# Decode step with cached attention beside a gated MLP: w4 loaded between the last V and wo, the gate folded into the head outputs, the second branch added on the PE

## Chip, cores, metric

One core of one Trainium2 chip. The metric is the device time of one execution in microseconds (us), lower is better. Every time below is of a run within 1.5% of the fastest of the same kernel. Kernels of one group of experiments ran on the same chip and share the runs of the kernel before.

## The reference, cut to what matters

```python
x = A_x                                                 # 2 x 1 x 1024, bf16
g = sigmoid((x * gate_w).sum(-1, keepdims=True))
# A: one query per head over a cache; B=2, H=32, Sk=16384, Dh=128
q = (x @ wq) as 32 heads
p = softmax(q . k_cache * Dh**-0.5)
a = (p . v_cache) as 4096 columns @ wo                  # wo 4096 x 1024
# B: a mixer and an MLP on the same x
x1 = x + shift(gelu(layernorm(x) @ w1)) @ w2            # 1024 x 1024 each
b  = x1 + gelu(layernorm(x1) @ w3) @ w4                 # w3 1024 x 3584, w4 3584 x 1024
return g * a + (1 - g) * b
```

The two caches are 268 MB each, the weights together 36 MB. Every byte is read once, and the output is 4 KB.

## The kernel before

All large loads go through one pool of three buffers of 64 KB per partition. A step of the attention (one batch element, two heads) takes one 8 MB K tile and one 8 MB V tile, 32 of each. The weights of the second branch take a turn in the same ring after steps 4, 8 and 16; wo comes last, in pieces.

```python
const = ctx.enter_context(tc.tile_pool(name="const", bufs=1))
big = ctx.enter_context(tc.tile_pool(name="big", bufs=NBIG))        # NBIG = 3
tpool = ctx.enter_context(tc.tile_pool(name="tpool", bufs=2))
# ... more pools behind them ...
V_SPLIT_LAST = [NJ // 2, NJ // 4, NJ // 8, NJ // 8]                 # NJ = 256
WO_SPLIT = [4] * 6 + [2, 2, 1, 1, 1, 1]                             # rows of wo, 256 KB each
# ...
def wo_stage():
    Q1 = const.tile([P, B, 32], BF16)
    # ... transposes OT, permutes it on the PE into Q (also a const tile) ...
    for r in range(32):
        for c in range(KC):                                         # KC = 8
            nc.tensor.matmul(wo_acc[:, c, :], lhsT=wo[:, r, :, c], rhs=Q[:, :, r],
                             start=(r == 0 and c == 0), stop=(r == 31 and c == KC - 1))
# ...
def st_down():                                                      # at step 16
    nc.vector.tensor_tensor(out=pre[:], in0=x1[:], in1=linear("w4", h2T)[:], op=ALU.add)
    nc.vector.tensor_tensor(out=pre[:], in0=pre[:], in1=over_r(omg_bc[:]), op=ALU.mult)
# ... the end:
fin = const.tile([P, KC, B], FP32)
nc.vector.tensor_tensor(out=fin[:], in0=wo_acc[:], in1=over_r(g_bc[:]), op=ALU.mult)
out_pm = const.tile([P, B, KC], BF16)
nc.vector.tensor_tensor(out=out_pm[:].rearrange("p b r -> p r b"), in0=fin[:], in1=pre[:], op=ALU.add)
```

Pools lie behind one another in each partition, in the order in which they are opened.

Of the kernel before, what the change touches and what calls it, by code (L numbers as in the profile page):

```python
# [10 lines left out]
FP32 = mybir.dt.float32  # L11
BF16 = mybir.dt.bfloat16
ACTF = mybir.ActivationFunctionType
ALU = mybir.AluOpType
# [9 lines left out]
def kernel(  # L24
# [15 lines left out]
    nc = tc.nc  # L40
    P = nc.NUM_PARTITIONS
    B, Sq, D = A_x.shape
# [3 lines left out]
    G = 2  # L46
    NJ = G * Sk // P
# [4 lines left out]
    KC = D // P  # L52
    FC = F // P
    scale = float(Dh) ** -0.5
    NHG = H // G
    NT = B * NHG
# [3 lines left out]
    const = ctx.enter_context(tc.tile_pool(name="const", bufs=1))  # L60
    big = ctx.enter_context(tc.tile_pool(name="big", bufs=NBIG))
# [8 lines left out]
    def misc_psum(shape, dtype=FP32):  # L70
        return mps.tile(shape, dtype, tag="misc", name="misc")

    def big_tile(name):
        return big.tile([P, SLOT], BF16, tag="big", name=name)
# [7 lines left out]
    kn_tiles = {}  # L82
    vn_tiles = {}
    wt = {}
    V_SPLIT_LAST = [NJ // 2, NJ // 4, NJ // 8, NJ // 8]

    def cache_rows(cache, i):
        b, hg = tiles[i]
# [11 lines left out]
    def load_v(i):  # L100
# [3 lines left out]
        j0 = 0  # L104
        for n in V_SPLIT_LAST if i == NT - 1 else [NJ]:
            nc.sync.dma_start(out=tv[:, j0 : j0 + n, :], in_=src[:, j0 : j0 + n, :])
# [3 lines left out]
    def load_rows(keys, srcs):  # L110

        t = big_tile("wt")
        c0 = 0
        for key, src in zip(keys, srcs):
            R, N = src.shape[0] // P, src.shape[1]
            v = t[:, c0 : c0 + R * N].rearrange("p (r n) -> p r n", n=N)
            nc.sync.dma_start(out=v, in_=src.rearrange("(p r) n -> p r n", p=P))
            wt[key] = v
            c0 += R * N


    WO_SPLIT = [4] * 6 + [2, 2, 1, 1, 1, 1]

    def load_wo():
        t = big_tile("wo")[:].rearrange("p (r n) -> p r n", n=D)
        src = A_wo.rearrange("(p r) n -> p r n", p=P)
        r0 = 0
        for n in WO_SPLIT:
            nc.sync.dma_start(out=t[:, r0 : r0 + n, :], in_=src[:, r0 : r0 + n, :])
            r0 += n  # L130
        wt["wo"] = t


    x_pm = const.tile([P, B, KC], BF16)
# [2 lines left out]
    def load_first():  # L137
# [7 lines left out]
    ident_f = const.tile([P, P], FP32)  # L145
# [4 lines left out]
        out=perm[:].rearrange("k (h a) -> k h a", a=4),  # L150
        in_=ident_f[:].rearrange("k (a h) -> k h a", a=4),
# [24 lines left out]
    for g in range(1, 4):  # L176
        nc.vector.tensor_tensor(
            out=osel_f, in0=osel_f, in1=ident_f[:, 40 * g : 40 * g + 8], op=ALU.add
# [4 lines left out]
    for v in range(4):  # L183
        nc.gpsimd.affine_select(
            out=selv[:, v],
            in_=selv[:, v],
# [21 lines left out]
    def total(src):  # L208

        ps = misc_psum([P, src.shape[1]])  # L210
        nc.tensor.matmul(ps[:], lhsT=ones_f[:], rhs=src, start=True, stop=True)  # L211
        return ps

    def over_r(v):

        return v.unsqueeze(1).to_broadcast([P, KC, B])


    g_bc = const.tile([P, B], FP32)
# [62 lines left out]
    OT = const.tile([P, B, H], BF16)  # L282
    wo_acc = acc.tile([P, KC, B], FP32, name="wo_acc")
# [56 lines left out]
    def pv_rows(V, PT, oc):  # L340



        O = ops.tile([P, 4 * Dh], FP32, name="O")
        for m in range(NM):
            for g in range(4):
                j0 = m * CJ + 4 * g
                nc.tensor.matmul(  # L348
                    O[32 * g : 32 * g + 32, :],
                    lhsT=PT[:, m : CJ * 32 : 16],  # L350
                    rhs=V[:, j0 : j0 + 4, :],
                    start=(m == 0),
                    stop=(m == NM - 1),
                )
        Os = ppool.tile([P, 4, Dh], FP32, tag="PrOs", name="Os")
        nc.scalar.copy(out=Os[:].rearrange("p x d -> p (x d)"), in_=O[:])  # L356
        for x in range(4):
            nc.tensor.matmul(  # L358
                oc[:], lhsT=Os[:, x, :], rhs=osel[:, x, :], start=(x == 0), stop=(x == 3)
            )  # L360

    def pv_stage(i):
        b, hg = tiles[i]
        PT = PT_tiles.pop(i)
        rs = rs_tiles.pop(i)
        V = vn_tiles.pop(i)[:].rearrange("p (j d) -> p j d", d=Dh)
        rs2 = stat.tile([P, G], FP32, name="rs2")
        nc.vector.tensor_scalar(  # L368
            out=rs2[:], in0=hmask[:], scalar1=rs[:, 0:1], scalar2=None, op0=ALU.mult
        )  # L370
        rinv = stat.tile([P, G], FP32, name="rinv")
        nc.vector.reciprocal(out=rinv[:], in_=total(rs2[:])[:])  # L372
        oc = misc_psum([P, G])
        pv_rows(V, PT, oc)
        nc.vector.tensor_tensor(  # L375
            out=OT[:, b, hg * G : (hg + 1) * G], in0=oc[:], in1=rinv[:], op=ALU.mult
        )

    def wo_stage():


        Q1 = const.tile([P, B, 32], BF16)
        for b in range(B):
            nc.vector.transpose(out=Q1[:, b, :], in_=OT[:, b, :])
        q_ps = misc_psum([P, B, 32])
        nc.tensor.matmul(q_ps[:], lhsT=perm[:], rhs=Q1[:], start=True, stop=True)
        Q = const.tile([P, B, 32], BF16)
        nc.vector.tensor_copy(out=Q[:], in_=q_ps[:])
        wo = wt.pop("wo").rearrange("k r (p c) -> k r p c", c=KC)
        for r in range(32):  # L390
            for c in range(KC):
                nc.tensor.matmul(
                    wo_acc[:, c, :],
                    lhsT=wo[:, r, :, c],
                    rhs=Q[:, :, r],
                    start=(r == 0 and c == 0),
                    stop=(r == 31 and c == KC - 1),
                )
# [38 lines left out]
    def linear(key, actT):  # L437

        w = wt.pop(key)
        R, C = w.shape[1], w.shape[2] // P  # L440
        ps = misc_psum([P, C, B])
        for c in range(C):
            for r in range(R):
                nc.tensor.matmul(  # L444
                    ps[:, c, :],
                    lhsT=w[:, r, :].rearrange("k (p c) -> k p c", c=C)[:, :, c],
                    rhs=actT[:, r, :],
                    start=(r == 0),
                    stop=(r == R - 1),
                )  # L450
        return ps
# [4 lines left out]
    x1 = const.tile([P, KC, B], FP32)  # L456
    xn2T = const.tile([P, KC, B], BF16)
    h2T = const.tile([P, FC, B], BF16)
    pre = const.tile([P, KC, B], FP32)
# [17 lines left out]
        gelu(h2[:], h2T[:], FC)  # L477

    def st_down():
        nc.vector.tensor_tensor(out=pre[:], in0=x1[:], in1=linear("w4", h2T)[:], op=ALU.add)  # L480
        nc.vector.tensor_tensor(out=pre[:], in0=pre[:], in1=over_r(omg_bc[:]), op=ALU.mult)


# [1 line left out]
    extra = {  # L485
        NT // 8: (lambda: load_rows(["w1", "w2"], [B_w1, B_w2]), st_mix),
        NT // 4: (lambda: load_rows(["w3"], [B_w3]), st_up),
        NT // 2: (lambda: load_rows(["w4"], [B_w4]), st_down),
    }
    xfers = [("big", "q", load_first)]  # L490
    steps = [("q", compute_q), ("gate", compute_gate)]

    for i in range(-1, NT):
        if i + 1 < NT:
            xfers.append(("big", f"k{i + 1}", lambda i=i: load_k(i + 1)))
            steps.append((f"k{i + 1}", lambda i=i: (build_z(i + 1), qk_stage(i + 1))))
        if i >= 0:
            xfers.append(("big", f"v{i}", lambda i=i: load_v(i)))
            steps.append((f"v{i}", lambda i=i: pv_stage(i)))
        if i + 1 < NT:  # L500
            steps.append(("", lambda i=i: softmax_stage(i + 1)))
        if i in extra:
            xfers.append(("big", f"x{i}", extra[i][0]))
            steps.append((f"x{i}", extra[i][1]))

    xfers.append(("big", "wo", load_wo))
    steps.append(("wo", wo_stage))

    ring_size = {"big": NBIG}
# [14 lines left out]
    for name, run in steps:  # L524
# [2 lines left out]
        done.add(name)  # L527
    assert not xfers

    fin = const.tile([P, KC, B], FP32)  # L530
    nc.vector.tensor_tensor(out=fin[:], in0=wo_acc[:], in1=over_r(g_bc[:]), op=ALU.mult)
    out_pm = const.tile([P, B, KC], BF16)
    nc.vector.tensor_tensor(
        out=out_pm[:].rearrange("p b r -> p r b"), in0=fin[:], in1=pre[:], op=ALU.add
    )
    with nc.allow_non_contiguous_dma(reason="4 KB"):
        nc.sync.dma_start(out=out.rearrange("b s (p r) -> p (b s) r", p=P), in_=out_pm[:])

# [29 lines left out]
```

## Time and profile before

| | before |
|---|---|
| time, median of the first three runs | 1342.54 us (1342.47 to 1343.81) |
| span of the profiled run | 1340.6 us |
| moved by DMA | 573.36 MB, mean 428 GB/s |
| share of the span busy: 16 DMA engines on the load queue, PE, DVE | 99.0%, 63%, 53% |

Lines of the profile's page. The GB/s line has 40 equal slices of the span; the queue lines give packets, MB and the share of the 16 engines' time.

```profile
span 1340.6 us, 12993 instructions
PE 845.7 (63%) x5587; PEld 402.6 (30%) x5587; DVE 707.6 (53%) x864; ACT 45.5 (3%) x100; POOL 14.4 (1%) x45
...
GB/s 405 437 435 435 434 423 437 425 437 439 429 432 426 437 435 437 431 433 431 421 437 440 432 435 433 432 427 437 431 431 437 429 433 433 437 431 439 433 412 277
DMA packets 12841, 573.36 MB, mean 428 GB/s; under 512 B 2032, under 2 KB 2032, under 8 KB 2800
...
q1 hardware_dynamic: 12784, 572.54, 99.0%
q8 instruction: 43, 0.70, 0.2%
q14 instruction: 14, 0.11, 0.0%
```

The DMA bounds the kernel: its engines are busy throughout, and only the last two slices fall off. Queues 8 and 14 are the fetching of instructions, in packets of 16 KB and of 8 KB, over engines that also carry the load.

The timeline's end, chosen lines (start in us, duration in us, engine, line, operation, out<-in, count, and in brackets the idle time before it and what ended it):

```profile
start us, us, engine line op out<-in xcount [idle before <-releaser]
...
1296.62 29.47 SPq L129 DMA_DIRECT2D wo<-in_A_wo_dram  x12
...
1320.51 9.86 PE L392 MATMUL wo_acc<-Q,wo 128*128 128x2 bf16 x160 [0.32 <-DVE Q L388]
...
1330.77 5.93 PE L392 MATMUL wo_acc<-Q,wo 128*128 128x2 bf16 x96 [0.39 <-DMA wo<-in_A_wo_dram]
1336.74 0.17 DVE L531 TENSOR_TENSOR fin<-wo_acc,g_bc 128x16 f32<-128x16 f32 x1 [16.28 <-PE wo_acc L392]
1336.95 0.23 DVE L533 TENSOR_TENSOR out_pm<-fin,pre 128x16 bf16<-128x16 f32 x1
1337.20 0.40 SPq L537 DMA_DIRECT2D out_dram<-out_pm  x1
```

PE starts wo late (its data has been landing since 1318.3), has caught up after 160 matmuls, waits 0.39 us for the piece with rows 20 to 23, and runs the last 96 matmuls without a gap: 5.93 us, 61.8 ns each.

The trace also records 16 completion increments for each transfer, one per DMA engine. First and last of the 16, for some transfers of the kernel before, in us:

```
transfer             first     last    last - first
first K tile         41.94    43.66     1.72
a tile near 120     119.34   121.23     1.88
a tile near 727     726.67   732.58     5.91
w4                  743.60   749.52     5.92
wo, rows 20 to 23  1319.96  1330.72    10.76
wo, row 31         1327.91  1335.87     7.96
```

The first increments of neighbouring 8 MB tiles are 19.35 us apart all the way (w4, 7 MB: 16.93), so the fastest engines never lacked work. And the engines drift apart: seven stay within about a microsecond of one another, and nine fall behind in steps: eight by about 1.55 us at a time, one by about 1 us at a time, and this one ends farthest behind, at 10.8 us. The kernel ends when the slowest engine has moved its share.

### The profile page before, as it was taken

To read this page: it belongs to the slowest core of one execution; us is meant where nothing else is said; L and a number is where in the kernel's file an instruction comes from. 1 tells how busy PE (TensorE), PEld (TensorE's weight loads), DVE (VectorE), ACT (ScalarE), POOL (GpSimd) and SP (SyncE) were. 2 spreads that over 40 slices of the span, in tenths; PEclk is the share of its full clock that TensorE was granted. 3 is DMA by queue.
4 is the path that set the end of the run, shared out by engine and by line. 5 is a ranking of instruction groups with operands and counts; after the bars stand their busy time and mean duration, and the time that the engine had idled before them with its cause. 6 is when DMAs were issued, how large, how long until landed. Compare 5 with 4: busy or idle time off the path is not lost.

```text
span 1340.6 us, 12993 instructions
## 1 busy us (share of the span) xinstructions
PE 845.7 (63%) x5587; PEld 402.6 (30%) x5587; DVE 707.6 (53%) x864; ACT 45.5 (3%) x100; POOL 14.4 (1%) x45
## 2 busy tenths in 40 slices
PE   2577656577657765555766577656556765555677
PEld 2233222433225322222322433222223322222336
DVE  0666565366651665545565166655455655445560
ACT  0000000000000000000000000000000000000000
POOL 0000000000000000000000000000000000000000
PEclk9988877688776877778887588777788877778885
DMA  9999999999999999999999999999999999999996
GB/s 405 437 435 435 434 423 437 425 437 439 429 432 426 437 435 437 431 433 431 421 437 440 432 435 433 432 427 437 431 431 437 429 433 433 437 431 439 433 412 277
DMA packets 12841, 573.36 MB, mean 428 GB/s; under 512 B 2032, under 2 KB 2032, under 8 KB 2800
## 3 DMA queue, kind: packets, MB, share of 16 engines
q1 hardware_dynamic: 12784, 572.54, 99.0%
q8 instruction: 43, 0.70, 0.2%
q14 instruction: 14, 0.11, 0.0%
HBM read 572.53 MB, written 0.00 MB: 427 GB/s over the span
## 4 chain that ended last, share of the span: by engine, by line
PE 27%; DVE 22%; DMA 22%; another core or an unknown queue 13%; issue 13%; ACT 2%; SPq 0%; ACTq 0%; POOL 0%
DVE T L296 19%; DMA Kn<-in_A_k_cache_dram 17%; PE S L304 13%; PE O L348 7%; DMA Vn<-in_A_v_cache_dram 3%; PE misc L444 3%; PE misc L358 2%; PE misc L211 2%; DMA wo<-in_A_wo_dram 2%; ACT Pr L332 1%; DVE PT L336 1%; ACT Os L356 1%; DVE mx L325 1%; DVE mdiag L318 1%
## 5 line engine op out<-in xcount | busy, mean ns | idle before, releaser
L304 PE MATMUL S<-T,z 128*128 128x512 bf16 x2048 | 597.6, 425 | 326.1 <-DVE T L296 310.6
L296 DVE STREAM_TRANSPOSE T<-Kn 128x1024 f32<-128x1024 f32 x512 | 612.0, 1229 | 267.4 <-DMA Kn<-in_A_k_cache_dram 217.6
L304 PEld LDWEIGHTS <-z 128*128 128x128 bf16 x2048 | 219.0, 107 | 699.2 <-issue 538.3
L348 PE MATMUL O<-Vn,PT 128*32 128x512 bf16 x2048 | 121.2, 389 | 2.7 <-DMA Vn<-in_A_v_cache_dram 2.7
L348 PEld LDWEIGHTS <-PT 128*32 128x32 bf16 x2048 | 73.8, 140 | 48.9 <-issue 20.0
L375 DVE TENSOR_TENSOR OT<-misc,rinv 128x2 bf16<-128x2 f32 x32 | 5.1, 159 | 156.8 <-PE misc L358 156.8
L211 PE MATMUL misc<-rs,ones_f 128*128 128x2 f32 x64 | 17.7, 346 | 76.4 <-DVE rs L368 76.4
L356 ACT COPY Os<-O 128x512 f32<-128x512 f32 x32 | 18.7, 585 | 1086.2 <-PE O L348 1086.2
L358 PE MATMUL misc<-osel,Os 128*128 128x2 f32 x256 | 34.5, 257 | 22.2 <-ACT Os L356 22.2
L358 PEld LDWEIGHTS misc<-osel,Os 128*128 128x128 f32 x256 | 31.8, 195 | 37.1 <-ACT Os L356 37.1
L315 DVE TENSOR_REDUCE m<-S 128x1 f32<-128x512 f32 x32 | 22.1, 691 | 36.9 <-PE S L304 36.9
L444 PEld LDWEIGHTS <-wt 128*128 128x128 bf16 x576 | 35.8, 172 | 18.5 <-DMA wt<-in_B_w_dram 17.2
L211 PEld LDWEIGHTS misc<-rs,ones_f 128*128 128x128 f32 x64 | 15.9, 309 | 81.1 <-issue 78.4
L336 DVE STREAM_TRANSPOSE PT<-Pr 128x512 bf16<-128x512 bf16 x32 | 22.8, 711 | 28.7 <-ACT Pr L332 28.7
L332 ACT ACTIVATE Pr<-S,nb 128x512 bf16<-128x512 f32 x32 | 22.0, 687 | 124.1 <-DVE nb L327 121.2
L211 PE MATMUL misc<-mdiag,ones_f 128*128 128x128 f32 x64 | 15.6, 325 | 15.6 <-DVE mdiag L318 15.6
L325 DVE TENSOR_REDUCE mx<-misc 64x1 f32<-64x64 f32 x64 | 14.2, 222 | 19.0 <-PE misc L211 18.6
L274 POOL TENSOR_TENSOR z<-qsel,own 128x32 bf16<-128x32 bf16 x32 | 10.7, 334 | 1226.0 <-PE S L304 1194.8
L249 PE MATMUL misc<-xT,wt 128*128 128x2 bf16 x256 | 7.1, 165 | 25.8 <-DVE xT L244 23.1
L444 PE MATMUL misc<-xn2T,wt 128*128 128x2 bf16 x224 | 14.4, 202 | 8.5 <-DMA wt<-in_B_w_dram 8.5
L444 PE MATMUL misc<-h2T,wt 128*128 128x2 bf16 x224 | 13.6, 198 | 8.3 <-DMA wt<-in_B_w_dram 8.3
L372 DVE RECIPROCAL rinv<-misc 128x2 f32<-128x2 f32 x32 | 5.4, 170 | 22.0 <-PE misc L211 22.0
(74 smaller groups left out, 106.6 us busy)
## 6 DMA issues: line engine op xcount, KB each, us to landing
wt<-in_B_w_dram SPq DMA_DIRECT2D x2, 7168.0 KB, 50.7
wo<-in_A_wo_dram SPq DMA_DIRECT2D x6, 1024.0 KB, 23.5
wt<-in_B_w_dram SPq DMA_DIRECT2D x2, 2048.0 KB, 39.4
Vn<-in_A_v_cache_dram SPq DMA_DIRECT2D x1, 4096.0 KB, 42.0
Vn<-in_A_v_cache_dram SPq DMA_DIRECT2D x1, 2048.0 KB, 46.5
Vn<-in_A_v_cache_dram SPq DMA_DIRECT2D x2, 1024.0 KB, 50.5
wo<-in_A_wo_dram SPq DMA_DIRECT2D x2, 512.0 KB, 18.0
wo<-in_A_wo_dram SPq DMA_DIRECT2D x4, 256.0 KB, 12.8
```

The source lines that it names most:

```text
L211: nc.tensor.matmul(ps[:], lhsT=ones_f[:], rhs=src, start=True, stop=True)
L296: nc.vector.transpose(out=T[:].rearrange("p w j s -> p j w s"), in_=Kw[:, m * CW : (m + 1) * CW].rearrange("p (j w e) -> p j w e", w=2, e=32),
L304: nc.tensor.matmul(S[:], lhsT=z[:, v, NM - 1 - m : NM - 1 - m + P], rhs=Tb[:, v // 2, :, v % 2], start=(m == 0 and v == 0), stop=(m == NM ...
L315: nc.vector.reduce_max(out=m[:], in_=S[:], axis=AX.X)
L318: nc.vector.tensor_scalar(out=mdiag[:], in0=ident_f[:], scalar1=m[:, 0:1], scalar2=None, op0=ALU.mult)
L325: nc.vector.reduce_max(out=mx[pa, :], in_=mall[pa, pa], axis=AX.X)
L332: nc.scalar.activation(out=Pr[:], in_=S[:], func=ACTF.Exp, bias=nb[:], scale=scale, accum_out=rs[:])
L336: nc.vector.transpose(out=PT[:], in_=Pr[:])
L348: nc.tensor.matmul(O[32 * g : 32 * g + 32, :], lhsT=PT[:, m : CJ * 32 : 16], rhs=V[:, j0 : j0 + 4, :], start=(m == 0), stop=(m == NM - 1),)
L356: nc.scalar.copy(out=Os[:].rearrange("p x d -> p (x d)"), in_=O[:])
L358: nc.tensor.matmul(oc[:], lhsT=Os[:, x, :], rhs=osel[:, x, :], start=(x == 0), stop=(x == 3))
L444: nc.tensor.matmul(ps[:, c, :], lhsT=w[:, r, :].rearrange("k (p c) -> k p c", c=C)[:, :, c], rhs=actT[:, r, :], start=(r == 0), stop=(r == ...
```

## The change

The intent: w4's load and PE work move from the middle to the end, where the last attention step (V product, copy, head outputs, transposes) can hide behind w4's transfer. Then wo's matmuls should not start late. The gate is multiplied into the head outputs, and the second branch is added to the output sums by an identity matmul, so that one conversion is left after the last matmul in place of two operations.

```diff
-    V_SPLIT_LAST = [NJ // 2, NJ // 4, NJ // 8, NJ // 8]
+    V_SPLIT_LAST = [NJ // 2, NJ // 2]
...
+    W4_SPLIT = [7] * 4
     WO_SPLIT = [4] * 6 + [2, 2, 1, 1, 1, 1]
-    def load_wo():
+    def load_pieces(key, weights, split):        # the same loop, for w4 and wo
...
-        nc.vector.tensor_tensor(
-            out=OT[:, b, hg * G : (hg + 1) * G], in0=oc[:], in1=rinv[:], op=ALU.mult
+        nc.vector.scalar_tensor_tensor(
+            out=OT[:, b, hg * G : (hg + 1) * G], in0=oc[:],
+            scalar=g_bc[:, b : b + 1], in1=rinv[:], op0=ALU.mult, op1=ALU.mult,
         )
...  in wo_stage
         for r in range(32):
+            if r == 24:
+                nc.tensor.matmul(
+                    wo_acc[:].rearrange("p c b -> p (c b)"), lhsT=ident_f[:],
+                    rhs=pre[:].rearrange("p c b -> p (c b)"), start=False, stop=False,
+                )
...  st_down: linear("w4", h2T) written out, rows outermost, to follow the pieces
-        NT // 2: (lambda: load_rows(["w4"], [B_w4]), st_down),
...
-    xfers.append(("big", "wo", load_wo))
+    xfers.append(("big", "w4", lambda: load_pieces("w4", B_w4, W4_SPLIT)))
+    steps.append(("w4", st_down))
+    xfers.append(("big", "wo", lambda: load_pieces("wo", A_wo, WO_SPLIT)))
...
-    fin = const.tile([P, KC, B], FP32)
-    nc.vector.tensor_tensor(out=fin[:], in0=wo_acc[:], in1=over_r(g_bc[:]), op=ALU.mult)
     out_pm = const.tile([P, B, KC], BF16)
-    nc.vector.tensor_tensor(
-        out=out_pm[:].rearrange("p b r -> p r b"), in0=fin[:], in1=pre[:], op=ALU.add
-    )
+    nc.vector.tensor_copy(out=out_pm[:].rearrange("p b r -> p r b"), in_=wo_acc[:])
```

(In the fold of the gate and in the matmul calls of this excerpt, arguments are joined on fewer lines than in the file. In the excerpts, here and below, comments that only explain are added.)

More of the change, by code (lines that the diff above doesn't have):

```diff
@@ L119, in load_rows @@
             c0 += R * N
+    W4_SPLIT = [7] * 4
     WO_SPLIT = [4] * 6 + [2, 2, 1, 1, 1, 1]
-    def load_wo():
-        t = big_tile("wo")[:].rearrange("p (r n) -> p r n", n=D)
-        src = A_wo.rearrange("(p r) n -> p r n", p=P)
+    def load_pieces(key, weights, split):
+        t = big_tile(key)[:, : sum(split) * D].rearrange("p (r n) -> p r n", n=D)
+        src = weights.rearrange("(p r) n -> p r n", p=P)
         r0 = 0
-        for n in WO_SPLIT:
+        for n in split:
             nc.sync.dma_start(out=t[:, r0 : r0 + n, :], in_=src[:, r0 : r0 + n, :])
             r0 += n
-        wt["wo"] = t
+        wt[key] = t
     x_pm = const.tile([P, B, KC], BF16)
@@ L374, in pv_stage @@
         pv_rows(V, PT, oc)
-        nc.vector.tensor_tensor(
-            out=OT[:, b, hg * G : (hg + 1) * G], in0=oc[:], in1=rinv[:], op=ALU.mult
+        nc.vector.scalar_tensor_tensor(
+            out=OT[:, b, hg * G : (hg + 1) * G],
+            in0=oc[:],
+            scalar=g_bc[:, b : b + 1],
+            in1=rinv[:],
+            op0=ALU.mult,
+            op1=ALU.mult,
         )
@@ L390, in wo_stage @@
         for r in range(32):
+            if r == 24:
+                nc.tensor.matmul(
+                    wo_acc[:].rearrange("p c b -> p (c b)"),
+                    lhsT=ident_f[:],
+                    rhs=pre[:].rearrange("p c b -> p (c b)"),
+                    start=False,
+                    stop=False,
+                )
             for c in range(KC):
@@ L479, in st_down @@
     def st_down():
-        nc.vector.tensor_tensor(out=pre[:], in0=x1[:], in1=linear("w4", h2T)[:], op=ALU.add)
+        w4 = wt.pop("w4").rearrange("k r (p c) -> k r p c", c=KC)
+        ps = misc_psum([P, KC, B])
+        for r in range(FC):
+            for c in range(KC):
+                nc.tensor.matmul(
+                    ps[:, c, :],
+                    lhsT=w4[:, r, :, c],
+                    rhs=h2T[:, r, :],
+                    start=(r == 0 and c == 0),
+                    stop=(r == FC - 1 and c == KC - 1),
+                )
+        nc.vector.tensor_tensor(out=pre[:], in0=x1[:], in1=ps[:], op=ALU.add)
         nc.vector.tensor_tensor(out=pre[:], in0=pre[:], in1=over_r(omg_bc[:]), op=ALU.mult)
```

## The prediction

> **What bounds it now.** The DMA. The page shows 573.36 MB over 1340.6 us, the 16 engines busy 99.0% of the span, and no slice before the last two under 405 GB/s; PE is busy 63%, DVE 53%. The trace's completion increments (16 per transfer, one per engine; the Trainium skill, "DMA: Bandwidth & Descriptors", "Why a DMA increments its semaphore by 16 and not by 1", says the engines finish independently, and these records agree) show more: the first increments of successive 8 MB transfers are 19.35 us apart from start to finish, so the queue never ran dry, and the spread from first to last engine grows from 1.9 us at 120 us to 10.8 us for wo. It grows in steps of about 1 us, as the 43 instruction-fetch packets of 16 KB (about 1.05 us each) do. So the end is: the slowest engine works through all its bytes, then a short rest.
>
> **The tail now.** The timeline: V31 lands at 1315.8, the wo matmuls start at 1320.5, behind the data, and have caught up at 1330.4, where PE waits 0.39 us for the sixth piece (rows 20 to 23, landed 1330.72). Then 96 matmuls run without a gap in 5.93 us (61.8 ns each; the skill, "TensorE: Matmul & The Clock Gate", "Back-to-back issue gap", gives about 62 ns per MATMUL for the sequencer, and the trace agrees). They end at 1336.7, 0.85 us after the last landing (1335.87). Two DVE operations (0.19 and 0.23 us), then the output DMA.
>
> **What the change does.**
> - Bytes and their order per engine: same total. w4's 7 MB (16.93 us between landings) leaves the middle, where the queue never ran dry and its 13.6 us of PE work held up no transfer, and comes before wo. Worth 0.
> - Three more pieces for w4, two fewer for V31; a piece costs about 0.07 us (first-engine landings of the 1 MB pieces against bulk): +0.1 us.
> - wo's issue waits for V30's head product, an estimated 1284 us after the shift of 17 us, with V31 and w4 (15 MB, 36 us) queued: no starvation. The last pieces' issue waits on earlier landings exactly as now.
> - V31's product, softmax and the transposed outputs hide behind w4's load. But w4's last piece lands near 1316, its 56 matmuls end near 1319.4 and wo starts there, 1 us earlier than now; PE had caught up anyway. Worth 0.
> - The gate in the head outputs: the same 32 DVE instructions, some 20 ns more each, off the path.
> - The identity matmul (two fp32 passes, about 0.23 us each at this clock as the head-output matmuls show) stands at row 24, in the gapless run of 96 matmuls: +0.45 us.
> - Two final DVE operations become one: -0.2 us.
>
> Net: about +0.3 us, on the end only.
>
> **Prediction.** 1342.8 us, 1341.0 to 1344.8 eight times in ten; faster by over 2%: 0.01, within: 0.98, slower: 0.01.
>
> **Signs.** DMA still 99%, last wo landing within 1.5 us of 1335.9, spread near 10.8 us; the slices around 750 us as full as their neighbours; PE waits for the sixth wo piece, then runs to the end in about 6.4 us; one DVE operation after it; the chain of waits ends in wo's DMA, PE, one DVE operation.
>
> **What would make it wrong.** Fetch packets meeting the slowest engine more or less often: 1 us each, both ways. The new issue order starving the queue (wo issued after 1310) would cost microseconds. If the 14 us w4 stage in the middle had cost the queue time that landings hide, up to that would be gained, but the increments say no. A faster clock through denser PE work would gain at most 0.8 us.

## The result, and the profile after

| | before | after |
|---|---|---|
| time, median | 1342.64 us (1342.47 to 1343.81, 4 runs) | 1338.47 us (1338.32 to 1338.53, 4 runs) |
| span of the profiled run | 1340.6 us | 1336.7 us |
| last landing of wo (all 16 engines) | 1335.87 | 1331.84 |
| end of PE, read as the start of the DVE operation that waits for it | 1336.74 | 1333.28 |

The ratio is 0.9968, 95% interval 0.9953 to 0.9982. Ratios are the mean time of one kernel's fast runs over that of the other's of the same rounds, so not quite the ratio of the medians quoted. The change is 0.3% faster: within 2%, but outside the predicted range of 1341.0 to 1344.8, and in the direction opposite to the predicted +0.3 us.

The page of the changed kernel:

```profile
span 1336.7 us, 12996 instructions
PE 845.2 (63%) x5589; PEld 403.1 (30%) x5589; DVE 709.2 (53%) x863; ACT 45.6 (3%) x100; POOL 14.2 (1%) x45
...
GB/s 409 436 436 434 422 440 434 429 440 434 422 435 437 440 436 422 430 440 428 438 438 433 430 432 430 440 438 426 434 430 438 438 432 430 434 428 436 434 421 294
DMA packets 12986, 573.37 MB, mean 429 GB/s; under 512 B 2048, under 2 KB 2048, under 8 KB 2816
...
q1 hardware_dynamic: 12928, 572.54, 99.1%
q8 instruction: 44, 0.72, 0.2%
q14 instruction: 14, 0.11, 0.0%
```

The engines are as busy as before and moved the same bytes in less time. The timeline's end:

```profile
start us, us, engine line op out<-in xcount [idle before <-releaser]
...
1280.76 41.45 SPq L130 DMA_DIRECT2D wo<-in_A_wo_dram  x12
...
1312.15 3.54 PE L498 MATMUL misc<-h2T,w 128*128 128x2 bf16 x56 [0.66 <-DMA w<-in_B_w_dram]
1315.56 6.01 PE L406 MATMUL wo_acc<-Q,wo 128*128 128x2 bf16 x96
...
1326.80 2.10 PE L406 MATMUL wo_acc<-Q,wo 128*128 128x2 bf16 x32 [0.35 <-DMA wo<-in_A_wo_dram]
1328.76 0.59 PE L398 MATMUL wo_acc<-pre,ident_f 128*128 128x16 f32 x2
1329.19 4.05 PE L406 MATMUL wo_acc<-Q,wo 128*128 128x2 bf16 x64
1333.28 0.23 DVE L557 CAST out_pm<-wo_acc 128x16 bf16<-128x16 f32 x1 [17.16 <-PE wo_acc L406]
1333.54 0.40 SPq L559 DMA_DIRECT2D out_dram<-out_pm  x1
```

The tail is what the prediction drew: PE waits for the sixth piece of wo and then needs 6.44 us, the identity matmul included. Seen from the last landing, PE ends *later* than before: 1333.28 - 1331.84 = 1.44 us after it, against 1336.74 - 1335.87 = 0.87. So the tail did not bring the gain. The landings did: the last one came 4.03 us earlier. The increments show where. Neighbouring 8 MB tiles are 19.32 us apart instead of 19.35, and the spread at rows 20 to 23 of wo is 9.2 us instead of 10.8.

The trace records each DMA packet. By size, mean duration in ns:

| packet | before | after |
|---|---|---|
| 64 KB of load | 2426.4 | 2422.7 |
| 32 KB of load | 1220.3 | 1216.9 |
| 8 KB of load | 314.8 | 309.7 |
| 16 KB instruction fetch | 1063.1 | 927.4 |

A packet of load takes some 4 ns less, whether it carries 8 KB or 64 KB. Of the 64 KB packets of before, 47% took 2420 ns, 19% took 2427 and 12% took 2418; in the changed kernel 97% took 2418. In the build, one thing differs for all of them: without the 64 bytes of `fin` in `const` the big buffers start at byte 20736 of each partition, a multiple of 256 (81 x 256), and not at 20800.

### The profile page after: what moved, and what is told of

Read it like the earlier page. It is cut to its first block, busy times and chain, and to the rows that moved or that the text cites. A ratio compares the mean times of both kernels' runs of the same rounds, so it can differ in the third digit from the quotient of the medians.

```text
span 1336.7 us, 12996 instructions
## 1 busy us (share of the span) xinstructions
PE 845.2 (63%) x5589; PEld 403.1 (30%) x5589; DVE 709.2 (53%) x863; ACT 45.6 (3%) x100; POOL 14.2 (1%) x45
## 4 chain that ended last, share of the span: by engine, by line
PE 29%; DVE 24%; DMA 17%; another core or an unknown queue 14%; issue 13%; ACT 3%; SPq 0%; ACTq 0%; POOL 0%
DVE T L297 20%; PE S L305 15%; DMA Kn<-in_A_k_cache_dram 13%; PE O L349 7%; PE misc L212 2%; PE misc L359 2%; DMA w<-in_B_w_dram 2%; DMA wo<-in_A_wo_dram 2%; PE misc L458 2%; ACT Pr L333 1%; DVE PT L337 1%; ACT Os L357 1%; DVE mx L326 1%; DVE mdiag L319 1%
## 5 line engine op out<-in xcount | busy, mean ns | idle before, releaser
L376 DVE SCALAR_TENSOR_TENSOR OT<-misc,g_bc,rinv 128x2 bf16<-128x2 f32 x32 | 7.0, 220 | 159.2 <-PE misc L359 159.2
L458 PEld LDWEIGHTS <-wt 128*128 128x128 bf16 x352 | 22.3, 165 | 9.8 <-DMA wt<-in_B_w_dram 8.5
L406 PE MATMUL wo_acc<-Q,wo 128*128 128x2 bf16 x256 | 16.3, 199 | 1.1 <-DMA wo<-in_A_wo_dram 1.1
```

The lines of the kernel that those rows point to most:

```text
L458: nc.tensor.matmul(ps[:, c, :], lhsT=w[:, r, :].rearrange("k (p c) -> k p c", c=C)[:, :, c], rhs=actT[:, r, :], start=(r == 0), stop=(r == ...
```

## The experiments

Theory A (address): the gain comes from the start of the big buffers, through the removed 64 bytes of `fin`. Rival B (tail): it comes from the work hidden or removed at the end. Rival C (chance): the reordered PE stream puts the instruction fetches where they delay the slowest engine less.

### before_fin_moved: the address alone

```diff
-    fin = const.tile([P, KC, B], FP32)
+    fin = t_tile([P, KC, B], FP32, "fin")       # a pool behind the big buffers
```

> The kernel before with one edit: the 64-byte tile fin stands in a pool behind the three big buffers, so that the buffers start 64 bytes lower in each partition (byte 20736, a multiple of 256, as in the changed kernel; before: 20800, 64 above one). No instruction and no order changes. Address theory: 1338.2 us, 8 KB packets 309 ns, fetch packets near 0.93 us. Tail theory (the gain is the work hidden and removed at the end): 1342.6 us, as before. Chance theory (other stretches of the stream met by fetches): 1342.6 give or take 1.

Measured: 1339.05 us (1338.50 to 1339.89) against 1342.81 on the same chip; ratio 0.9972, interval 0.9959 to 0.9984. The 8 KB packets took 310.0 ns in the mean, the fetches 938.9. Theory A holds in size (the median is 0.85 us above its 1338.2); B and C said no change.

```profile
start us, us, engine line op out<-in xcount [idle before <-releaser]
...
1326.69 5.93 PE L392 MATMUL wo_acc<-Q,wo 128*128 128x2 bf16 x96 [0.21 <-DMA wo<-in_A_wo_dram]
1332.66 0.17 DVE L531 TENSOR_TENSOR fin<-wo_acc,g_bc 128x16 f32<-128x16 f32 x1 [15.97 <-PE wo_acc L392]
1332.87 0.23 DVE L533 TENSOR_TENSOR out_pm<-fin,pre 128x16 bf16<-128x16 f32 x1
1333.12 0.40 SPq L537 DMA_DIRECT2D out_dram<-out_pm  x1
```

This end of its timeline is the one of before, shifted by 4.08 us: the same 5.93 us of PE and the same two DVE operations.

### after_pad64: the change without the address

```diff
+    pad = const.tile([P, 32], BF16, name="pad")     # 64 bytes, never read
+    nc.vector.memset(pad[:], 0.0)
```

> The changed kernel with an unused 64-byte tile, so that the big buffers start at byte 20800 again. Address theory: 1342.9 us (before plus the 0.3 of the prediction). Tail theory: 1338.5 us.

Measured: 1342.44 us (1342.21 to 1343.39); ratio to before 0.9998, interval 0.9986 to 1.0011. The whole change at the old address is worth nothing measurable. Its timeline's end can be laid beside that of before, since the data arrive at the same times (last landing 1335.86 and 1335.87):

```profile
start us, us, engine line op out<-in xcount [idle before <-releaser]
...
1315.88 3.54 PE L500 MATMUL misc<-h2T,w 128*128 128x2 bf16 x56 [0.78 <-DMA w<-in_B_w_dram]
1319.28 6.16 PE L408 MATMUL wo_acc<-Q,wo 128*128 128x2 bf16 x96
...
1330.75 2.09 PE L408 MATMUL wo_acc<-Q,wo 128*128 128x2 bf16 x32 [0.39 <-DMA wo<-in_A_wo_dram]
1332.70 0.59 PE L400 MATMUL wo_acc<-pre,ident_f 128*128 128x16 f32 x2
1333.13 4.05 PE L408 MATMUL wo_acc<-Q,wo 128*128 128x2 bf16 x64
1337.22 0.23 DVE L559 CAST out_pm<-wo_acc 128x16 bf16<-128x16 f32 x1 [17.38 <-PE wo_acc L408]
1337.48 0.40 SPq L561 DMA_DIRECT2D out_dram<-out_pm  x1
```

wo starts at 1319.28 instead of 1320.51, and that buys nothing, because PE waits at 1330.7 for the same piece in both. The identity matmul then lengthens the gapless end, and the saved DVE operation gives part of that back. The output DMA is issued at 1337.48 instead of 1337.20: +0.28 us, close to the +0.3 that the prediction summed up. Its +0.1 us for the added piece does not show: the last landings are 0.01 us apart.

### after_gap64: transfers or engines

```diff
+    gap = ctx.enter_context(tc.tile_pool(name="gap", bufs=1))     # between big and tpool
     tpool = ctx.enter_context(tc.tile_pool(name="tpool", bufs=2))
...
+    pad = gap.tile([P, 32], BF16, name="pad")
+    nc.vector.memset(pad[:], 0.0)
```

> The changed kernel with the unused 64 bytes behind the big buffers: these stay on a multiple of 256, every tile behind them (transposes, probabilities, statistics) moves to 64 above one. If the destination of the transfers is what counts: 1338.5 us. If it is the alignment of the tiles the engines write and read: near 1342.5 us.

Measured: 1338.63 us (1338.33 to 1338.71), ratio 0.9968. The big buffers count, not the tiles behind them. This kernel is also the changed kernel on the chip of before_fin_moved, and the two differ by 0.4 us (1338.63 and 1339.05) with overlapping ranges.

### after_q_moved, after_q1_moved, after_pad32: which multiple

```diff
  after_q_moved   -  Q1 = const.tile([P, B, 32], BF16)      +  Q1 = t_tile([P, B, 32], BF16, "Q1")
                  -  Q = const.tile([P, B, 32], BF16)       +  Q = t_tile([P, B, 32], BF16, "Q")
  after_q1_moved  the first of the two lines only
  after_pad32     the pad of after_pad64, with 32 bytes
```

> The changed kernel with the two 128-byte tiles Q1 and Q moved behind the big buffers, which then start at byte 20480, a multiple of 512 too (the changed kernel: 20736, a multiple of 256 only). If 256 is the step that counts: 1338.5 us. If a larger power of two still gains: 1336 us or so.

> The changed kernel with the tile Q1 (128 bytes) behind the big buffers, which then start at byte 20608, 128 above a multiple of 256. If 256 is the step that counts: 1342.5 us. If 128 is: 1338.5 us. If the cost grows with the distance: 1346 us.

> The changed kernel with an unused 32-byte tile: the big buffers start 32 bytes above a multiple of 256 (byte 20768). If every start off a multiple of 256 costs one more piece per packet: 1342.5 us, as at 64. If the cost grows with the distance: 1340.5 us.

| kernel | start of the big buffers | above a multiple of 256 | time, us | before, same chip | ratio (95%) |
|---|---|---|---|---|---|
| after_q_moved | 20480 | 0 (and of 512) | 1338.58 | 1342.81 | 0.9969 (0.9955 to 0.9982) |
| after_gap64 | 20736 | 0 | 1338.63 | 1342.81 | 0.9968 (0.9956 to 0.9981) |
| after_pad32 | 20768 | 32 | 1343.09 | 1342.39 | 1.0005 (0.9992 to 1.0018) |
| after_pad64 | 20800 | 64 | 1342.44 | 1342.81 | 0.9998 (0.9986 to 1.0011) |
| after_q1_moved | 20608 | 128 | 1342.27 | 1342.39 | 0.9999 (0.9986 to 1.0011) |

At the starts tried it is a yes or no: on a multiple of 256 or not. 128 is not enough, 512 brings nothing more, and the distance does not matter. The Trainium skill fits here in part, "DMA: Bandwidth & Descriptors", section "How a descriptor splits into AXI transactions": a descriptor is cut into transactions of 256 bytes, and one that starts off such a boundary gets its first transaction from the boundary below. The step of 256 agrees. The page also counts the bytes skipped at the front as fetched and paid for, so that a start farther off would cost more; the 64 KB packets here do not show that (2427.0, 2425.9 and 2425.9 ns in the mean at 32, 64 and 128 bytes off). The page names no duration for it and does not speak of the SBUF side. That the extra transaction is what costs the 4 ns is an inference; no run here looked inside an engine.

### before_halves, before_halves_fin_moved: per packet or per byte

```diff
  load_k
-        nc.sync.dma_start(
-            out=t[:].rearrange("p (j d) -> p j d", d=Dh), in_=cache_rows(A_k_cache, i)
-        )
+        tv = t[:].rearrange("p (j d) -> p j d", d=Dh)
+        src = cache_rows(A_k_cache, i)
+        for j0 in (0, NJ // 2):
+            nc.sync.dma_start(out=tv[:, j0 : j0 + NJ // 2, :], in_=src[:, j0 : j0 + NJ // 2, :])
  load_v
-        for n in V_SPLIT_LAST if i == NT - 1 else [NJ]:
+        for n in V_SPLIT_LAST if i == NT - 1 else [NJ // 2, NJ // 2]:
```

The second kernel has the edit of before_fin_moved as well.

> The kernel before with each K and V tile loaded by two transfers of half the length, so that a packet carries 32 KB per partition in place of 64 and there are twice as many; the buffers stay at 64 above a multiple of 256. From the 32 KB and 64 KB packets of before (mean 1220.3 and 2426.4 ns): 2 x 1220.3 - 2426.4 = 14.2 ns more per 64 KB, 8 of them per engine and tile, 64 tiles: 7.3 us, about 1350 us.

> The same halves with fin moved, so that the buffers start on a multiple of 256. If the start costs some 4 ns per packet whatever its length, the gain of the move grows with the number of packets, from the 3.8 us of before_fin_moved to about 6: about 1344 us. If it costs per byte, the gain stays 3.8: about 1346 us.

Measured on one chip: 1347.05 us (1347.01 to 1347.78) and 1341.23 us (1340.96 to 1341.47), before 1342.71. Both absolute expectations were nearly 3 us too high. They were worked out from the few 32 KB packets of before (mean 1220.3 ns); the many of before_halves took 1218.5, which accounts for 1.8 us of the first miss; the rest is open. The question asked was the difference, and that came out: 5.82 us with twice the packets, 3.76 without, so the cost is per packet. The increments agree: first increments of neighbouring 4 MB transfers are 9.715 and 9.682 us apart in the mean, 0.033 us lost per 4 MB, where before and before_fin_moved (19.352 and 19.318) lose 0.034 per 8 MB.

### after_ident8, after_fine_end: the tail, tested by itself

```diff
  both             -            if r == 24:     +            if r == 8:
  after_fine_end   -    WO_SPLIT = [4] * 6 + [2, 2, 1, 1, 1, 1]
                   +    WO_SPLIT = [4] * 5 + [2] * 4 + [1] * 4
```

> The changed kernel with the identity matmul at row 8 of wo, where PE waits for data anyway, in place of row 24. Theory: its 0.45 us leave the gapless end; 1338.0 us, and PE ends 0.45 us nearer to the last landing (0.95 us after it; 1.4 in the changed kernel). Rival: it costs nothing where it stands; 1338.5 us.

> As after_ident8, and the sixth piece of wo (rows 20 to 23) in two pieces of two rows, so that PE need not wait for four rows with eight more to come. Theory: PE ends 0.55 us after the last landing, 0.8 us earlier than in the changed kernel; 1337.7 us, the fastest of all. Rival: the extra piece's own cost and its later issue take it back; 1338.5 us.

Measured: 1338.61 us (1337.89 to 1338.76; ratio 0.9971) and 1338.13 us (1337.97 to 1338.73; ratio 0.9969), before 1342.39. The timings separate neither kernel from the other or from the changed kernel (0.9968). A timeline is finer. The end of after_ident8 (last landing 1331.88), then of after_fine_end (last landing 1331.97):

```profile
start us, us, engine line op out<-in xcount [idle before <-releaser]
...
1326.87 5.95 PE L406 MATMUL wo_acc<-Q,wo 128*128 128x2 bf16 x96 [0.39 <-DMA wo<-in_A_wo_dram]
1332.85 0.23 DVE L557 CAST out_pm<-wo_acc 128x16 bf16<-128x16 f32 x1 [16.70 <-PE wo_acc L406]
```

```profile
start us, us, engine line op out<-in xcount [idle before <-releaser]
...
1324.46 8.21 PE L406 MATMUL wo_acc<-Q,wo 128*128 128x2 bf16 x128 [0.35 <-DMA wo<-in_A_wo_dram]
1332.71 0.23 DVE L557 CAST out_pm<-wo_acc 128x16 bf16<-128x16 f32 x1 [16.50 <-PE wo_acc L406]
```

From the last landing to the end of PE it is 1.44 us in the changed kernel, 0.97 with the identity matmul early and 0.74 with the finer pieces as well. The first step is as expected (0.45 us). The second fell short of the expected 0.55: PE now waits for rows 16 to 19 and then has 128 matmuls to do, 8.2 us, while the rest of the data needs 7.5. The median of after_fine_end is the lowest of all kernels, but the runs do not show it to be faster than the changed kernel.

## Why the prediction was wrong

**The step that failed** is the size given to the bulk of the load. The prediction put it as "Bytes and their order per engine: same total" and let the bulk time stand: 19.35 us per tile, 1.05 us per fetch packet, last landing near 1335.9. Nothing in its sum was allowed to touch the 1330 us of loading. It counted the removed `fin` only as a DVE operation ("Two final DVE operations become one: -0.2 us"), not as 64 bytes in front of the big buffers. Those 64 bytes were the result: moving `fin` alone gives 3.76 us between medians on its chip (the whole change: 4.17 on another), and giving the bytes back takes the whole gain away.

**How 64 bytes make about 4 us**, from before and before_fin_moved:
- There are 624 load packets of 8 KB and more per engine (9984 in all over 16 engines). The 64 KB ones take 2426.4 and 2422.4 ns in the mean, so an estimate is 624 x 4.0 ns = 2.5 us. Between the first increment of the first K tile and that of rows 20 to 23 of wo, the measured difference is 1278.02 - 1275.45 = 2.57 us.
- The spread at those rows shrank from 10.76 to 9.45 us, by 1.31. The prediction took its steps of about 1 us for the 16 KB fetches of queue 8. The landings say otherwise: the slowest engine falls behind with the 8 KB packets of queue 14. In the kernel before, times in us:

```
packet of queue 14    last transfer landed before it    next one landed
starts at             at        last - first            at        last - first
 682.8                 673.56   5.02                     693.88   5.98
 941.1                 924.65   6.90                     944.98   7.86
1063.0                1061.10   7.87                    1081.43   8.86
1192.2                1178.17   8.82                    1198.49   9.79
1311.3                1309.90   9.86                    1313.32  10.78
```

  Between 944.98 and 1061.10 four fetches of queue 8 pass, and the spread stays at 7.86 to 8.01. In the mean, eleven of queue 14's 14 packets took 0.33 us, and the load packet behind each took 0.66 us longer than others of its size; in before_fin_moved it was 0.31 and 0.54. An estimate from these is a lag of 10.8 and of 9.3 us, 1.5 less. The other three packets lengthened the load packet behind them by less, 0.38 to 0.42 us in before. The records name no engine, so that the eleven fell to one engine is inferred from the steps.
- The 16 KB fetches took 1063.1 and 938.9 ns, 124 ns less. They set the other eight engines back, which end 7.7 to 9.4 us behind in before, so they are no part of this sum.
- Together 2.57 + 1.31 = 3.88 us; the first tile's landing was 0.20 us earlier besides. The last landing moved by 1335.87 - 1331.71 = 4.16.

Why the fetches of both queues, which do not write to the big buffers, become shorter is not settled. They did so in every kernel on a multiple of 256 (those of 16 KB: 927 to 939 ns) and in none off it (1056 to 1071 ns), so it goes with the address; sharing the engines with load packets may explain it, but no run took the two apart.

**Point by point, what held:**
- The DMA bounds the kernel, and the slowest engine sets the end: yes. The 4 us are a gain in its last landing.
- Taking w4 out of the middle is worth 0, and so is hiding the last attention step: shown for the two together by after_pad64, 0.9998 of before, with wo started 1.2 us earlier to no effect.
- The identity matmul in the gapless end costs 0.45 us: 0.45 in the chain of waits of the changed kernel, and 0.47 when after_ident8 moves it (1.44 - 0.97).
- wo issued near 1284, w4's matmuls ended near 1319.4, net +0.3 us: in after_pad64 1284.48, 1319.28 and +0.28.
- The gate in the head outputs: off the path, but 220 ns each against 159 on the page, 61 more and not 20.
- The expected signs "last wo landing within 1.5 us of 1335.9, spread near 10.8 us" failed, by 4.03 us and 1.5 us. They were the right signs to name, and they point straight at the failed step.
- "Fetch packets meeting the slowest engine more or less often" was named as a danger, but the number of fetch packets stayed (43 before and 44 after on queue 8, 14 and 14 on queue 14); what changed was how much each cost, and the slowest engine was set back by those of queue 14.

## What to carry to other kernels

When the DMA bounds a kernel, a change must also be judged by what it does to the tile addresses: look up the start of the load buffers in the built program before and after, and put them on a multiple of 256 bytes in the partition (open their pool first, or pad what lies ahead). The cost off it was about 4 ns per packet at lengths of 8 to 64 KB, so with packets of half the length it was paid twice as often. The few packets of 2 and 4 KB do not show it clearly (medians of 84 and 84 ns, 160 and 159 ns, in before and before_fin_moved). When a change gives an unexpected few tenths of a per cent throughout a run, separate its layout from its work by padding the layout back.

## What the Trainium skill lacked or had wrong

- "DMA: Bandwidth & Descriptors", "How a descriptor splits into AXI transactions", gives the 256-byte boundary but no time, and does not say that the start of the SBUF destination counts. Here destinations 32, 64 or 128 bytes off cost about 4 ns per packet (64 KB: 2426.4 against 2422.4 ns; 8 KB: 314.8 against 310.0), 3.8 us of 1342.8 in all.
- "SBUF — State Buffer", "Operand start alignment", says of itself that its runs are about legality and timed nothing. For DMA destinations the runs here add the speed: multiples of 256 and 512 alike (1338.6 us for both), everything below alike and slower (1342.3 to 1343.1).
- "Runtime: NRT & Kernel Launch", "Instruction fetch mechanics", gives no time that a fetch costs the engines of a load, and no other page that was found does. Here, in the kernel before, an engine falls behind by about 1.55 us with a fetch of 16 KB and by about 1 us with one of 8 KB, part of it in the load packet behind the fetch (0.50 and 0.66 us longer), and the slowest engine ends 10.8 us behind the fastest. The 16 KB fetches took 927 to 939 ns or 1056 to 1071 ns according to the start of the load buffers. Which engines these are, and how to spread the fetches, the trace did not tell.
